# Two single PSUM banks in place of two halves of one tile, in a pool opened anew for each part

## The chip, the cores and the metric

One NeuronCore of a Trainium2 chip runs the whole program. The metric is the device time of one execution in microseconds, the median of three runs.

## What is computed

The reference chains three stages. An attention over 32 memory slots comes first (8 batches, 8 heads, 576 tokens, head width 64); its result is the input of two feed-forward layers in a row.

```python
a = exp(phi - max over tokens); a = a / (sum over tokens + 1e-9)
k_m = einsum('bhsm,bhsd->bhmd', a, k);  v_m = einsum('bhsm,bhsd->bhmd', a, v)
attn = softmax(q @ k_m.T / 8);          x = attn @ v_m          # 4608 tokens x 512
h = x @ moe_w_in;   x = (h * sigmoid(h)) @ moe_w_out            # 512 -> 2048 -> 512
h = x @ moe2_w_in;  x = elu(h) @ moe2_w_out                     # 512 -> 2048 -> 512
```

## The kernel before

All products are made on TensorE (PE); ACT and DVE empty PSUM, form the operands (most numbers are split into two float16 halves, so that one product is three matmuls, `mm3`, L1092) and do the pointwise work. The program has three parts.

- **The first steps**: a list of step names written out by hand (`FIRST`, run in the loop at L1850 to L1853) handles the first batch: its attention, the first weights, its first products.
- **Part 1** (`plan_first`, to about 675 us): the other batches' attention and the first feed-forward layer. A small planner (`Plan`) orders its steps by priorities, readiness and a table of costs, when the program is built; on the chip each engine then runs its own list in that order, and semaphores hold an instruction until what it needs is there.
- **Part 2** (a second `Plan`, from about 675 us to the end): the second feed-forward layer over nine blocks of 512 tokens, i = 0 to 8. For each block `plan_in2` runs eight steps, q = 0 to 7, each of seven products of six matmuls, and `plan_out2` runs the output products in two halves, e = 0 and 1. The planner mixes the in-products of one block with the out-products of the block before.

PSUM has eight banks. `ps_m` holds two double tiles, m0 and m1, in four of them; the pool `ps_a` holds the other four: a single tile with the tag a, one with the tag c, and one double tile with the tag u of shape [128, 2, 512], one bank for each half. `pair_tile` makes such a double tile. In part 1 the double tile serves as a third place for products (`ps_half` with 2, the name ph) and for the two halves of one product (`u_mm`, the name up).

In the first steps and in part 2 the same four banks are used singly, in turn. `a_tile` (L134) counts requests in `turn[0]`; requests 0 and 2 of every four get a new tile with the tag a or c, requests 1 and 3 get a view of the first or second half of a double tile named `both`, which is made once at the start (L153) and once more when part 2 begins (L1857):

```python
        k = turn[0] % 4
        turn[0] += turn[1]
        if turn[1]:
            if k % 2:
                v = both[0][:, k // 2, :n]
```

So in part 2 `both` is one tile all along, whose halves are written and read again and again, while a and c are new tiles on each request.

In part 2 a block's in-products use four banks, and the out-products the other four (`bank_tile`, L1488; a ring of four). Ring 1 is the pool `ps_o`, with four buffers of one tag; it is opened when `ps_m` has been closed (`open_ps_o`, L1484). Ring 0 is `a_tile`. Blocks with even i have their in-products in ring 0, those with odd i in ring 1.

One step q of `plan_in2` asks for two banks: A for four products, which ACT empties (`copy_c`, L1528), and D for three, which DVE empties with an addition (`add_c`, L1532). In an even block A is a tile a or c, called h2A in the trace, and D is a half of `both`: the first half for even q, the second for odd q. In an odd block A and D are tiles of `ps_o`, called h2A and h2D. The order of the products, copies and additions within a step is the same for both. The second product into D (index 6, `p7`) starts a new sum in the bank, and so waits for the addition that read the first (`c11`). Steps q and q+1 overlap in the plan, so that the two banks called D are in use at the same time.

Of the kernel before, what the change touches and what calls it, by code (L numbers as in the profile page):

```python
# [9 lines left out]
F32 = mybir.dt.float32  # L10
# [6 lines left out]
PSUM = bass.MemoryType.PSUM  # L17

P = 128
# [76 lines left out]
def attn_moe_moe(ctx: ExitStack, tc: tile.TileContext, qT, phiT, kvm, kvt, w1i, w1o, w2i, w2o, out):  # L96
# [9 lines left out]
    ps_a = ctx.enter_context(tc.tile_pool(name="ps_a", bufs=4, space=PSUM))  # L106
# [27 lines left out]
    def a_tile(shape, name, tag="a"):  # L134

        k = turn[0] % 4
        turn[0] += turn[1]
        if turn[1]:
            if k % 2:
                n = int(np.prod(shape[1:]))  # L140
                v = both[0][:, k // 2, :n]
                return v if len(shape) == 2 else v.rearrange(
                    "p (a b) -> p a b", a=shape[1]) if len(shape) == 3 else v.rearrange(
                    "p (a b c) -> p a b c", a=shape[1], b=shape[2])
            tag = "ac"[k // 2]
        return ps_a.tile(shape, F32, tag=tag, name=name, bufs=1)

    both = []

    def pair_tile(name):  # L150
        return ps_a.tile([P, 2, 512], F32, tag="u", name=name, bufs=1)

    both.append(pair_tile("both"))  # L153

    def col(name, n=1):
        return const.tile([P, n], F32, name=name)
# [546 lines left out]
    def mem_T(b, g):  # L703

        z = st[b]
        if g < NG:
            ps = z["eT", g] = a_tile([P, NC - 1, P], "eT", "c")
            for c in range(NC - 1):
                nc.tensor.transpose(ps[:, c], z["phi"][:, g, TAIL * g + c * P:TAIL * g + (c + 1) * P], ident)
        else:  # L710
            ps = z["eT", g] = a_tile([P, P], "etail", "c")
            nc.tensor.transpose(ps, z["phi"].rearrange("p g s -> p (g s)")[:, S - TAIL:S + TAIL], ident)
# [15 lines left out]
    def mem_kv(b, g, c):  # L728
        z = st[b]
        if (g, c) == (0, 0):  # L730
            z["kvp"] = a_tile([P, NG, P], "kvp", "c")
        t = z.pop(("kv", g, c))
        last = c == NC - 1
        for g in range(NG) if last else (g,):
            for h in range(4):
                m = slice(32 * h, 32 * h + 32)
                nc.tensor.matmul(  # L737
                    z["kvp"][m, g],
                    es_tail[:, g, m] if last else z["es"][:, (NC - 1) * g + c, m],
                    t[:, h * P:(h + 1) * P],  # L740
                    start=(g == 0 and c == 0 or g == 1 and last),
                    stop=(g == 0 and last or g == 1 and c == NC - 2),
                    tile_position=(0, 32 * h),
                )
# [646 lines left out]
    def plan_weights(pl, after, h_free):  # L1391

        for q in range(NRES + NRING):
            wi_load[q] = pl.load(896, 1, lambda q=q: load_wi(q, f"wi{q}" if q < NRES else "wi"), after)
            if q >= NRES:
                pl.ring("wi", NRING)
                wi_free[q] = pl.take("wi", wi_load[q])
        for n, j in enumerate(ORDER):
            deps = pl.ring("wr", 3) if n < 3 else h_free[(n - 3) // 2]
            wq_load[j] = [None, None]  # L1400
            for e in range(2):
                wq_load[j][e] = pl.load(512, 2, lambda n=n, e=e: load_wq(n, e), deps + wq_load[j][:e] + after)
            if n < 3:
                pl.take("wr", wq_load[j][0])
# [17 lines left out]
    def scale_tiles():  # L1422
        for name in ("mb", "mx", "am", "p_x", "pxw", "s_x", "s_g", "tmp"):
            sc[name] = ph2.tile([P, NB], F32, tag=name, name=name)
        for name in ("inv2", "io2"):
            sc[name] = ph2.tile([P, NB, 2], F32, tag=name, name=name)

    def x2_scales(a, e):


        n = e - a
        lo = [i * TB // S for i in range(a, e)]
        hi = [((i + 1) * TB - 1) // S for i in range(a, e)]
        mb, m, am, t = sc["mb"], sc["mx"], sc["am"], sc["tmp"]
        nb = hi[-1] + 1 - lo[0]
        nc.vector.tensor_reduce(out=mb[:, :nb], in_=mx_x2[:, lo[0]:lo[0] + nb], axis=AX.X, op=ALU.add)
        two_of = sum(u < v for u, v in zip(lo, hi))
        if two_of:
            tt(m[:, :two_of], mb[:, :two_of], mb[:, 1:two_of + 1], ALU.max)
        if two_of < n:  # L1440
            nc.vector.tensor_copy(m[:, two_of:n], mb[:, two_of:n])
        nc.gpsimd.partition_all_reduce(am[:, :n], m[:, :n], P, bass_isa.ReduceOp.max)
        r = slice(a, e)
        pow2sq(sc["p_x"][:, r], am[:, :n], t[:, :n])
        scaled_recip(sc["s_x"][:, r], sc["p_x"][:, r], 2.0 ** 12, t[:, :n])
        nc.vector.tensor_scalar(
            out=sc["pxw"][:, r], in0=sc["p_x"][:, r], scalar1=p_w2im, scalar2=None, op0=ALU.mult
        )
        scaled_recip(sc["s_g"][:, r], sc["pxw"][:, r], 2.0 ** 4, t[:, :n])
        for o, u, v, f in (("inv2", "p_x", p_w2i, 2.0 ** -24), ("io2", "pxw", p_w2o, 2.0 ** -16)):  # L1450
            for k in range(2):
                nc.vector.tensor_scalar(
                    out=sc[o][:, r, k], in0=sc[u][:, r], scalar1=v[:, k:k + 1], scalar2=f, op0=ALU.mult, op1=ALU.mult
                )

    def plan_x2(pl, i, rank):

        z = y[i]
        z["xh"] = [None] * (KD // 2)
        done = []  # L1460
        for k in range(KD // 2):
            load = pl.load(512, rank, lambda k=k: x2_tile(i, k), pl.ring("x", NX))
            free = pl.take("x", load)
            last = load
            for n in range(4):
                last = pl.add("DVE", COST["sum"], rank, lambda k=k, n=n: operands(z["x", k])[n](), [last])

            def hi(k=k):
                z["xh"][k] = ph2.tile([P, 2, 7, TQ], F16, tag=f"xh{k}", name=f"xh{i}_{k}")
                split_hi(z["xh"][k][:, 0], z["x", k][:, :B12], sc["s_x"][:, i:i + 1])  # L1470

            def lo(k=k):
                split_lo(z["xh"][k][:, 1], z["xh"][k][:, 0], z["x", k][:, :B12], sc["s_x"][:, i:i + 1])

            last = pl.add("ACT", COST["hi"], rank, hi, [last] + pl.ring(f"xh{k}", 1))
            z["xh_free", k] = pl.take(f"xh{k}", last)
            last = pl.add("DVE", COST["lo"], rank, lo, [last])
            free.append(last)
            done.append(last)
        z["xh_done"] = done  # L1480
# [367 lines left out]
    with tc.manual_schedule():  # L1848
        first = first_steps()
        turn[1] = 1  # L1850
        for name in FIRST.split():
            first.pop(name)()
        assert not first  # L1853
        turn[:] = 0, 0
        busy = plan_first()
        turn[1] = 1
        both[:] = [pair_tile("both")]  # L1857
        early.close()
        ph2 = ctx.enter_context(tc.tile_pool(name="ph2", bufs=1))
        scale_tiles()  # L1860
        nc.vector.tensor_reduce(out=p_w2im, in_=p_w2i, axis=AX.X, op=ALU.max)
        x2_scales(0, B - 1)
        pl = Plan(None, busy)
        last = st[B - 1]
        last["made"] = {}
        for n in range(NT):
            last["T_free", n] = pl.take("T", None)
        out1, squares, loads = plan_out1(
            pl, B - 1, 0, None, NT, {}, [], lambda: ph2.tile([P, 4, HS], F32, tag="y", name="y", bufs=2), ("y", 2), 1200)
        w1s_load = pl.gates["x"] = loads[4:5]  # L1870
        pl.gates[1] = [pl.add("PE", 0.0, 0, open_ps_o, out1)]
        for n in range(4, 7):
            pl.gates[f"t{5 + (tcount[0] + n) % NT}"] = last["T_free", n]
        made = last["made"]
        h_free = [made[T3, 0] + made[T3, 1] + made[T1, 0] + made[T1, 1], made[T4, 0] + made[T4, 1] + made[B22, 0] + made[B22, 1]]
        plan_x2(pl, 0, 0)
        plan_weights(pl, w1s_load, h_free)
        for i in range(NB):
            for q in range(KQ):
                plan_in2(pl, i, q)  # L1880
            plan_out2(pl, i, 0)
            if i == 2:
                pl.add("DVE", 2.5, 1000 * i + RANK["x2"], lambda: x2_scales(B - 1, NB), [y[i]["t_done", KQ - 1, 0]] + squares)
            if i + 1 < NB:
                plan_x2(pl, i + 1, 1000 * i + RANK["x2"])
            plan_out2(pl, i, 1)
        pl.run()
# [50 lines left out]
```

## Time and profile before

| | |
|---|---|
| median of three runs | 1367.56 us (1367.33 to 1369.19) |
| the profiled execution's own time | 1371.49 us |
| its span on the core | 1369.7 us |
| mean granted TensorE clock | 0.992 |
| PE busy | 97% of the span |
| DVE busy, ACT busy | 80%, 69% |
| part 2 | about 675 us to the end |

The span is the stretch from the first to the last instruction of one profiled execution; its own time is what a timer around that execution gives. A busy PE is one that has matmuls under way; the idle time in front of an instruction is put down to the semaphore event that came last. L1092 is the line of the helper `mm3`, which issues nearly all matmuls, so the rows are told apart by the tiles: out<-in, by the program's names without numbers, and `both` is the double tile whichever half is meant.

### The profile page before, as it was taken

Reading aid. Unit: us, or ns where it says so; the run is one execution under the profiler, and the core shown is the slowest. Engines: PE = TensorE matmul, PEld = TensorE weight load, DVE = VectorE, ACT = ScalarE, POOL = GpSimd, SP = SyncE. Lnnn points to the kernel's source line nnn. Section 1 sums busy time; section 2 is a strip of 40 time slices with the busy share of each in tenths; the row PEclk is TensorE's granted clock in tenths of the full one; section 3 lists DMA queues with packets and bytes.
Section 4 is the critical chain, followed back from the end, with each engine's and each line's share of the span. In section 5 each row is a group of like instructions: output and inputs, shape, how many; then the busy total and the mean of one; then the engine's idle time right before and its main releaser. Section 6 shows DMA issues by size and latency. Waiting matters only on the chain.

```text
span 1369.7 us, 28731 instructions
## 1 busy us (share of the span) xinstructions
PE 1335.2 (97%) x12089; PEld 1093.8 (80%) x12089; DVE 1102.5 (80%) x1731; ACT 951.1 (69%) x1374; POOL 85.3 (6%) x147
## 2 busy tenths in 40 slices
PE   8998999999999999999988999999999999999998
PEld 4676777777777776777877888888888888888887
DVE  7678887897979898898878696979787897869784
ACT  5767775868677796778486676858575867767672
POOL 0033100000001011011000000000000000000000
PEclk8999999999999999999999999999999999999999
DMA  9584777368657947635863151414232332414120
GB/s 390 192 265 137 268 277 271 120 234 276 209 198 236 335 145 256 241 135 200 346 215 112 53 172 44 152 50 147 74 124 85 113 112 77 148 43 166 58 97 32
DMA packets 65601, 233.07 MB, mean 170 GB/s; under 512 B 8896, under 2 KB 15040, under 8 KB 60864
## 3 DMA queue, kind: packets, MB, share of 16 engines
q1 hardware_dynamic: 52992, 187.19, 40.0%
q0 software_dynamic: 12480, 44.05, 8.5%
q8 instruction: 94, 1.54, 0.5%
q14 instruction: 35, 0.29, 0.1%
HBM read 186.12 MB, written 40.89 MB: 166 GB/s over the span
## 4 chain that ended last, share of the span: by engine, by line
PE 86%; DMA 5%; DVE 4%; ACT 3%; issue 1%; SPq 0%; POOL 0%; ACTq 0%; DVEq 0%; POOLq 0%
PE ph L1092 30%; PE o L1092 17%; PE h2A L1092 13%; PE both L1092 12%; PE h2D L1092 4%; PE up L930 2%; PE ph L1099 2%; PE ph L1138 2%; DMA w1i_hl<-w1i_hl 1%; PE sc L833 1%; DVE h L1532 1%; PE kvp L737 1%; DMA kv<-in_kvm 1%; DMA wi<-w2is 1%; DMA q<-in_qT 1%
## 5 line engine op out<-in xcount | busy, mean ns | idle before, releaser
L1092 PEld LDWEIGHTS <-wi 128*128 128x128 f16 x3024 | 296.2, 98 | 52.9 <-issue 13.2
L1092 PEld LDWEIGHTS <-wq 128*128 128x128 f16 x3024 | 295.7, 98 | 38.2 <-issue 3.7
L1092 PE MATMUL ph<-T,w1s 128*128 128x288 f16 x2352 | 302.0, 286 | 0.1
L1092 PEld LDWEIGHTS <-w1s 128*128 128x128 f16 x2352 | 227.5, 98 | 62.4 <-issue 6.5
L1092 PE MATMUL o<-t,wq 128*128 128x256 f16 x2160 | 273.2, 273 | 0.5 <-DVE t L206 0.4
L1092 PE MATMUL h2A<-xh,wi 128*128 128x256 f16 x1728 | 229.1, 274 | 5.3 <-DMA wi<-w2is 3.7
L1528 ACT ACTIVATE h<-h2A,inv 128x256 f32<-128x256 f32 x288 | 133.5, 469 | 141.3 <-PE h2A L1092 137.9
L206 DVE SCALAR_TENSOR_TENSOR t<-h,s_g,t 128x768 f16<-128x768 f32 (+1 forms) x144 | 163.7, 1146 | 10.1 <-ACT t L201 9.7
L1092 PE MATMUL ph<-aT,u 128*128 128x288 f16 x1344 | 167.3, 286 | 1.7 <-ACT h L1175 1.0
L201 ACT ACTIVATE t<-h,s_g 128x768 f16<-128x768 f32 (+1 forms) x144 | 146.4, 1034 | 24.8 <-DVE h L165 13.8
L1092 PEld LDWEIGHTS <-u 128*128 128x128 f16 x1344 | 130.9, 98 | 36.7 <-issue 3.9
L206 DVE SCALAR_TENSOR_TENSOR T<-h,c,T 128x1152 f16<-128x1152 f32 x98 | 137.5, 1413 | 22.9 <-ACT T L201 22.5
L165 DVE TENSOR_TENSOR h<-h 128x256 f32<-128x256 f32 (+1 forms) x302 | 129.4, 462 | 2.9
L201 ACT ACTIVATE T<-h,c 128x1152 f16<-128x1152 f32 x98 | 121.3, 1250 | 12.8 <-DVE h L165 7.0
L1092 PE MATMUL both<-t,wq 128*128 128x256 f16 x864 | 117.5, 272 | 1.5 <-DVE h L1532 1.2
L1532 DVE SCALAR_TENSOR_TENSOR h<-both,inv,h 128x256 f32<-128x256 f32 x120 | 56.8, 481 | 59.9 <-PE both L1092 52.0
L1092 PE MATMUL both<-xh,wi 128*128 128x256 f16 x720 | 96.2, 273 | 7.6 <-DVE h L1532 7.6
L1175 ACT ACTIVATE h<-ph,inv 128x576 f32<-128x576 f32 x112 | 81.9, 737 | 22.1 <-PE ph L1092 21.6
L1570 DVE SCALAR_TENSOR_TENSOR h<-e,h 128x1024 f32<-128x1024 f32 x72 | 87.7, 1218 | 7.1 <-ACT e L1566 7.1
L1563 ACT ACTIVATE e<-h 128x1024 f32<-128x1024 f32 x72 | 75.6, 1050 | 15.2 <-DVE h L1532 15.2
L1092 PE MATMUL h2D<-xh,wi 128*128 128x256 f16 x576 | 76.7, 273 | 0.0
L1566 ACT ACTIVATE e<-e 128x1024 f32<-128x1024 f32 x72 | 75.6, 1050 | 0.7
(214 smaller groups left out, 1437.9 us busy)
## 6 DMA issues: line engine op xcount, KB each, us to landing
w1s<-w1os SPq DMA_DIRECT2D x98, 512.0 KB, 4.5
wi<-w2is SPq DMA_DIRECT2D x56, 896.0 KB, 4.6
kv<-in_kvm SPq DMA_DIRECT2D x48, 256.0 KB, 5.4
q<-in_qT SPq DMA_DIRECT2D x32, 288.0 KB, 7.1
raw<-in_w1i SPq DMA_DIRECT2D x8, 1024.0 KB, 13.0
raw<-in_w1o SPq DMA_DIRECT2D x8, 1024.0 KB, 5.2
raw<-in_w2i SPq DMA_DIRECT2D x8, 1024.0 KB, 6.1
raw<-in_w2o SPq DMA_DIRECT2D x8, 1024.0 KB, 6.0
```

The source lines that it names most:

```text
L165: nc.vector.tensor_tensor(out=out, in0=a, in1=b, op=op)
L201: nc.scalar.activation(out=hi, in_=x, func=AF.Copy, scale=s)
L206: nc.vector.scalar_tensor_tensor(out=lo, in0=x, scalar=s, in1=hi, op0=ALU.mult, op1=ALU.subtract)
L930: nc.tensor.matmul(ps[c, :], z["vT"][:, i, g, c], wW[f][:, h % 2, 2 * g + h // 2], start=(i == 1), stop=(i == 0), tile_position=(0, 32 * h))
L1092: nc.tensor.matmul(o, w, x[:, c], start=first, stop=last, **how)
L1099: nc.tensor.matmul(o, w, x[:, c], start=(i == 0), stop=(i == n - 1))
L1175: nc.scalar.activation(out=h[m // KQ][:, :, m % KQ], in_=w.pop(m), func=AF.Silu, scale=z["inv1"][:, m // 4:m // 4 + 1])
L1528: nc.scalar.activation(out=w["x"][:, s], in_=w["A"], func=AF.Copy, scale=inv)
L1532: return pl.add("DVE", COST["add"], base, lambda: nc.vector.scalar_tensor_tensor(out=w["x"][:, s], in0=w["D"], scalar=inv, in1=w["x"][:, s ...
L1563: nc.scalar.activation(out=w["e"], in_=w["x"][:, B21:], func=AF.Relu, scale=-1.0)
L1566: nc.scalar.activation(out=w["e"], in_=w["e"], func=AF.Exp, scale=-1.0)
L1570: nc.vector.scalar_tensor_tensor(out=x, in0=w["e"], scalar=-1.0, in1=x, op0=ALU.add, op1=ALU.max)
```

## The change

The double tile leaves the pool `ps_a` for a pool of its own, `ps_u`, at the other end of PSUM. That pool is closed and opened anew for each part. In the first steps and in part 2 the requests 1 and 3 of `a_tile` now get new single tiles with the tags b and d from that pool, in place of a half of `both`; in part 1 the pool holds the double tile with the tag u as before. The order of the instructions, the planner's costs and the shapes stay as they are.

```diff
         k = turn[0] % 4
         turn[0] += turn[1]
+        pool = ps_a
         if turn[1]:
-            if k % 2:
-                n = int(np.prod(shape[1:]))
-                v = both[0][:, k // 2, :n]
-                return v if len(shape) == 2 else v.rearrange(
-                    "p (a b) -> p a b", a=shape[1]) if len(shape) == 3 else v.rearrange(
-                    "p (a b c) -> p a b c", a=shape[1], b=shape[2])
-            tag = "ac"[k // 2]
-        return ps_a.tile(shape, F32, tag=tag, name=name, bufs=1)
-
-    both = []
+            tag = "abcd"[k]
+            pool = ps_a if k % 2 == 0 else pair["pool"]
+        return pool.tile(shape, F32, tag=tag, name=name, bufs=1)
+
+    pair = {}
+
+    def open_pair():
+        if pair:
+            pair["open"].close()
+        pair["open"] = ctx.enter_context(ExitStack())
+        pair["pool"] = pair["open"].enter_context(tc.tile_pool(name="ps_u", bufs=1, space=PSUM, side="right"))
 
     def pair_tile(name):
-        return ps_a.tile([P, 2, 512], F32, tag="u", name=name, bufs=1)
-
-    both.append(pair_tile("both"))
+        return pair["pool"].tile([P, 2, 512], F32, tag="u", name=name, bufs=1)
+
+    open_pair()
...
         assert not first
         turn[:] = 0, 0
+        open_pair()
         busy = plan_first()
         turn[1] = 1
-        both[:] = [pair_tile("both")]
+        open_pair()
         early.close()
```

## Rows read from the trace of the kernel before

**Rows 1.** The page, busy time of the engines and their share of the span.

```profile
PE 1335.2 (97%) x12089; PEld 1093.8 (80%) x12089; DVE 1102.5 (80%) x1731; ACT 951.1 (69%) x1374; POOL 85.3 (6%) x147
```

**Rows 2.** The page, the chain that ended last, by engine.

```profile
PE 86%; DMA 5%; DVE 4%; ACT 3%; issue 1%; SPq 0%; POOL 0%; ACTq 0%; DVEq 0%; POOLq 0%
```

**Rows 3.** PE's waits by releaser in windows 675:755, 832:908, 984:1056: us, times, longest.

```profile
PE both L1092 <- DVE h L1532: 2.1, 4, 0.7
...
PE both L1092 <- DVE h L1532: 1.0, 2, 0.6
...
PE both L1092 <- DVE h L1532: 1.9, 3, 1.2
```

**Rows 4.** PE's waits in front of tile both, 670 us to the end: us, times.

```profile
  DVE h L1532: 8.7, 15
```

**Rows 5.** Windows 908:984 to 1132:1206: length, busy PE, PEld, DVE, ACT, POOL; PEclk.

```profile
908.00:984.00 76.00, 75.83 (x693) 67.56 (x692) 60.58 (x101) 53.46 (x77) 2.19 (x4) 1.00 0.31 102
984.00:1056.00 72.00, 70.12 (x637) 62.04 (x635) 59.06 (x99) 50.15 (x68) 2.18 (x4) 1.00 0.33 107
1056.00:1132.00 76.00, 76.00 (x697) 67.98 (x696) 61.73 (x102) 52.21 (x74) 2.17 (x4) 1.00 0.31 101
1132.00:1206.00 74.00, 72.11 (x655) 63.81 (x654) 59.63 (x99) 51.11 (x70) 2.18 (x4) 1.00 0.32 104
```

**Rows 6.** Groups of PE, 755 to 1282 us: count | busy us, mean ns | idle us, releaser.

```profile
L1092 PE MATMUL both<-t,wq 128*128 128x256 f16 x729 | 100.6, 272 | 0.9 <-DVE h L1532 0.6
L1092 PE MATMUL h2D<-xh,wi 128*128 128x256 f16 x576 | 76.7, 273 | 0.0
L1092 PE MATMUL both<-xh,wi 128*128 128x256 f16 x444 | 59.0, 272 | 4.2 <-DVE h L1532 4.2
```

**Rows 7.** Timeline around 1024 us: start, us, engine, line, tiles [idle before, releaser].

```profile
1022.46 0.82 PE L1092 MATMUL h2A<-xh,wi 128*128 128x256 f16 x6
...
1022.73 0.48 DVE L1532 SCALAR_TENSOR_TENSOR h<-both,inv,h 128x256 f32<-128x256 f32 x1 [0.81 <-PE both L1092]
...
1023.92 0.47 DVE L1532 SCALAR_TENSOR_TENSOR h<-both,inv,h 128x256 f32<-128x256 f32 x1
...
1024.45 0.82 PE L1092 MATMUL both<-xh,wi 128*128 128x256 f16 x6 [1.17 <-DVE h L1532]
```

**Rows 8.** The same timeline around 1031 us.

```profile
1030.54 0.48 DVE L1532 SCALAR_TENSOR_TENSOR h<-both,inv,h 128x256 f32<-128x256 f32 x1 [1.25 <-PE both L1092]
...
1031.61 0.48 DVE L1532 SCALAR_TENSOR_TENSOR h<-both,inv,h 128x256 f32<-128x256 f32 x1
...
1032.14 0.81 PE L1092 MATMUL both<-xh,wi 128*128 128x256 f16 x6 [0.33 <-DVE h L1532]
```

**Rows 9.** Timeline of the first steps, around 20 us and around 44 us.

```profile
18.25 0.69 DVE L165 TENSOR_TENSOR att<-both,smx 128x512 f32<-128x512 f32 x1
...
20.88 0.29 DVE L165 TENSOR_TENSOR att<-both,smx 128x128 f32<-128x128 f32 x1
...
21.23 1.08 PE L914 MATMUL both<-w1i,vT 64*32 64x256 f32 x8 [0.52 <-DVE att L165]
...
43.26 1.22 DVE L379 SCALAR_TENSOR_TENSOR w1i<-raw,w1i 128x1024 uint32<-128x1024 uint32 x1
...
44.91 0.15 PEld L914 LDWEIGHTS both<-w1i,vT 64*32 64x32 f32 x8 [0.39 <-DVE w1i L379]
```

**Rows 10.** The chain of block 0, in order of time: start, us, what.

```profile
718.77 0.67 PE both L1092 x6
719.46 6.66 DMA wi<-w2is
```

**Rows 11.** Timeline, PE's first product into a bank of `ps_o`.

```profile
698.60 0.82 PE L1092 MATMUL o<-t,wq 128*128 128x256 f16 x6
```

**Rows 12.** DMA issues, of the page and of 690:740: KB each, us to landing.

```profile
raw<-in_w1o SPq DMA_DIRECT2D x8, 1024.0 KB, 5.2
...
x2d<-y POOLq DMA_DIRECT2D x1, 576.0 KB, 11.2
```

## The prediction, made before the kernel was run

> **What bounds the kernel now.** I read the page's busy times first, then the chain, then PE's waits stretch by stretch. PE is busy for 97% of the span [rows 1] and makes up 86% of the chain that ended last [rows 2]. So a microsecond in which PE stands still is nearly a microsecond of the whole, and one saved on DVE or ACT is worth nothing unless PE waited for it. The change touches PSUM banks alone, so the question is which of PE's idle times hang on the double tile.
>
> In part 2 PE stood idle 15 times, 8.7 us in all, in front of a matmul into `both`, each time until a DVE addition of L1532 had ended [rows 4]. These waits fall into the even blocks, where D is a half of `both`: 2.1 us in block 0, 1.0 in block 2, 1.9 in block 4 [rows 3]; blocks 6 and 8 show the same 1.9 again, which adds up to 8.8 with the rounding, against the 8.7 of the one row. The odd blocks do the same products, copies and additions in the same order, with single tiles in their four banks, and 576 matmuls into h2D had 0.0 us of idle time in front of them; 444 matmuls of the same shape into `both` in the same stretch had 4.2 [rows 6]. The windows say it again: PE idles 1.9 us of 72 and 1.9 of 74 in the even blocks 4 and 6, and 0.2 and 0.0 of 76 in the odd blocks 3 and 5 [rows 5]. An odd block is thus a trial run of what the change makes of an even one.
>
> **Why the double tile waits.** Take the longest kind [rows 7]. PE ends its products into h2A at about 1023.28 (1022.46 + 0.82). Next in its list is step q = 6's second product into D, in the first half. The addition that empties that half runs from 1022.73 to 1023.21, so the bank is free before PE is. PE starts at 1024.45 all the same: it waits for the next addition, 1023.92 to 1024.39, which belongs to step 5 and reads the second half. Which half each side names is not in the rows; I read it from the kernel (even q, first half; odd q, second) and from the order of the instructions. I went through the 15 waits in this way: 12 wait for an addition that reads the other half, and for each of them the last reader of their own half was done by the time PE was free. So the wait hangs on the tile as a whole, not on the bank.
>
> The other three are the 0.33 us waits of blocks 4, 6 and 8 [rows 8]. There PE does wait for its own half (the addition at 1031.61), but that addition is late because the one before it, at 1030.54, had waited 1.25 us for a product into the other half. They go with the same cause.
>
> **The change, part by part.**
>
> - *Single tiles b and d in part 2.* Removes the 15 waits: 8.7 us [rows 4]. What is late next? In the odd blocks nothing is [rows 5, 6]; there DVE and ACT are busy for 61 and 52 to 53 us of 76 [rows 5], so they can follow a PE that comes a little sooner. In block 0 PE also waits for transfers of weights; the one on the chain is issued at 719.46, right after the products into `both` that end at 719.44 and free its buffer [rows 10], so it moves with PE and takes nothing back. I take all 8.7; the lower bound is the first rival's 8.7 - 3.5 - 2.1 = 3.1.
> - *Out-products in `both`.* Beside 0.6 us that is in the 8.7 already, 0.3 us of idle time stood before them between 755 and 1282 us [rows 6]. With single tiles I take the 0.3 as gone; bounds 0 and 0.3.
> - *Single tiles in the first steps.* One wait of the same kind, 0.52 us at 21.23: the matmul writes the half that the subtraction at 18.25 had read by 18.94, and waits for the one at 20.88, which reads the other half [rows 9]. What follows on PE moves along at most until 44.91, where a weight load waits for a conversion that ends at 44.48 [rows 9]; so about 0.4 us can be kept there, and later stretches of the chain are DMA [rows 2], which may not move. I take 0.2; bounds 0 and 0.4.
> - *Part 1.* The pool holds the double tile as before, and its waits stay. Nothing is gained or lost.
> - *Opening the pool twice.* The trace has one such event: `ps_m` is closed and `ps_o` opened in its banks, and PE's first product there has no idle time in front of it [rows 11]. The new tiles' banks were last read long before they are next written. I take 0. The upper bound is what still travels when a pool is opened: one load of first-layer weights, 5.2 us, at the first opening and one store of 11.2 us at the second [rows 12], 16.4 us together, if all engines had to wait for it. Nothing below 0 is possible, since no instruction goes away.
> - *Other banks.* Tiles move to other bank numbers. Matmuls of one shape last 272 or 273 ns in `both` and in h2D, which lie in different banks [rows 6]: 0. The granted clock is 1.00 in even and odd blocks alike [rows 5], the level of 2.4 GHz, so there is no term for it.
> - *Queues.* No instruction is moved past another, no DMA is added, no queue is reordered.
>
> Sum: 8.7 + 0.3 + 0.2 = 9.2 us off. The profiled execution took 1371.5 us, so it would take 1362.3; the median of the runs lies 3.9 us below it (its span is 1369.7), so the same 9.2 off the median of 1367.6 gives **1358.4 us**.
>
> **The rivals.**
>
> 1. *Part of the gain comes back as other waits.* At the three waits of 1.17 us in blocks 4, 6 and 8 DVE runs without a break from 1023.92 to past 1024.45 [rows 7]; if PE comes 1.2 us sooner and the next product then needs an addition that DVE has not reached, 3 x 1.2 = 3.5 us return. Block 0, which has few out-products to fill in with, may give back its 2.1 [rows 3], and the first steps their 0.2. What is left is 8.7 + 0.3 - 3.5 - 2.1 = 3.4, so 1364.2 us. The 0.0 in the odd blocks [rows 6] speaks against it; that block 0 has no odd counterpart speaks for it.
> 2. *Nothing changes, because the waits are a matter of too few banks.* The bubbles repeat, three to a block. Then four banks hold the next product up whichever tile they are cut from, and the change, which adds no bank, leaves 1367.6 us. The odd blocks speak against it: four banks, and 0.0 us of idle time [rows 6]. The Trainium skill's page "Perfetto Trace Analysis", section "Optimization Strategy", reads a gap that repeats on the engine that should be saturated as a possible lack of SBUF or PSUM for the next tile. By that rule the change is worth nothing; the trace does not agree with it for this gap.
> 3. *Slower: opening a pool holds the program up.* If each opening makes every engine wait until all that is under way has landed, it costs up to 5.2 + 11.2 = 16.4 us [rows 12], against 9.2 gained: 1374.8 us. The place is the end of the first steps and the start of part 2; it decides once the two openings cost more than 9.2 us together. [Rows 11] speak against it.
>
> **How the numbers follow.** The forecast gets 0.70, the first rival 0.16, the second 0.09, the third 0.05. The predicted time is the forecast's, 1358.4. The range begins at 1357.0, which is the forecast with all bounds at their best (8.7 + 0.3 + 0.4 = 9.4, so 1358.2) and 1.2 us for the scatter of the median (the three runs lie 1.9 us apart); it ends at 1364.5, just past the first rival. About 0.8 lies in it. A measurement of this kernel can tell some 0.2%, 2.7 us, from no change: faster means below 1364.8. The forecast and nearly all of the first rival lie there, 0.84; the second rival and the rest of the first make 0.11 for no change; the third makes 0.05 for slower.
>
> **What the profile of the changed kernel would show.** If right: no PE wait of more than 0.2 us in front of D's products in the even blocks (their tile is then called h2D there too, 1296 matmuls in all with about 0.0 idle), PE busy for all but some 0.2 us of each block from 2 on, the wait at 21 us gone, and part 2 starting at nearly the same time as before. The forecast is wrong if the same waits stand in front of the single tiles (second rival), if waits of PE for ACT, DVE or weights grow in the even blocks (first rival), or if PE or the DMA queues stand still around 60 us or 675 us (third rival).

## The result, and the profile after

The changed kernel takes 1353.80 us (median; four runs, 1351.77 to 1354.85) where the kernel before took 1367.45 us beside it: a ratio of 0.9896, with an interval from 0.9881 to 0.9912. That is 13.7 us less, where 9.2 had been forecast; the time lies below the range (1357.0 to 1364.5). The direction, the place and the cause were right, the size was not.

The profiled execution took 1354.85 us, with a span of 1353.1 and a mean granted clock of 0.995. The page's busy times and the chain by engine, which answer to [rows 1] and [rows 2]:

```profile
PE 1327.9 (98%) x12089; PEld 1092.9 (81%) x12089; DVE 1101.8 (81%) x1731; ACT 950.2 (70%) x1374; POOL 85.2 (6%) x147
```

```profile
PE 88%; DMA 4%; DVE 3%; ACT 3%; issue 1%; POOL 0%; SPq 0%; ACTq 0%; DVEq 0%; POOLq 0%
```

DVE and ACT do the same work as before to within 1 us. The 16.6 us by which this span is shorter than the one before are PE's: its waits, and 7 us of "busy" time, of which more below.

PE's matmuls into D, the group on the page (count | busy, mean ns | idle us in front), and all that PE waits for from 670 us on (us, times, longest), which answers to [rows 3, 4, 6]:

```profile
L1094 PE MATMUL h2D<-xh,wi 128*128 128x256 f16 x1296 | 174.1, 274 | 0.0
```

```profile
PE h2A L1094 <- DMA wi<-w2is: 4.1, 3, 2.1
PE h2A L1094 <- ACT h L1530: 1.0, 2, 0.6
```

All 1296 matmuls into D now go by the name h2D, and none shows idle time in front of it. The list of PE's waits has lost its longest entry, and no other has come in its place.

The windows of the even blocks 4 and 6, to be read beside [rows 5] (length, busy PE, PEld, DVE, ACT, POOL; PEclk):

```profile
970.00:1042.00 72.00, 72.00 (x661) 64.40 (x659) 59.26 (x99) 51.56 (x72) 2.18 (x4) 1.00 0.32 107
...
1116.00:1189.00 73.00, 73.00 (x672) 65.41 (x670) 59.85 (x101) 51.61 (x72) 2.18 (x4) 1.00 0.32 105
```

PE is busy in all of 72 and of 73 us, where 1.9 us were missing in each.

And the place of [rows 7], now at 1013 us (timeline: start, us, engine, line, tiles):

```profile
1012.50 0.48 DVE L1534 SCALAR_TENSOR_TENSOR h<-h2D,inv,h 128x256 f32<-128x256 f32 x1
...
1013.21 0.82 PE L1094 MATMUL h2A<-xh,wi 128*128 128x256 f16 x6
...
1013.69 0.48 DVE L1534 SCALAR_TENSOR_TENSOR h<-h2D,inv,h 128x256 f32<-128x256 f32 x1
1013.87 0.82 PE L1094 MATMUL h2D<-xh,wi 128*128 128x256 f16 x6
```

PE starts its six matmuls into h2D 0.66 us after the six into h2A, at 1013.87, while the addition that held it up before (1013.69 to 1014.17) is still under way: it reads another tile now.

### The profile page after: what moved, and what is told of

Same layout as the page of the kernel before. It is cut to its first block, busy times and chain, and to the rows that moved or that the text cites. A ratio compares the mean times of both kernels' runs of the same rounds, so it can differ in the third digit from the quotient of the medians.

```text
span 1353.1 us, 28725 instructions
## 1 busy us (share of the span) xinstructions
PE 1327.9 (98%) x12089; PEld 1092.9 (81%) x12089; DVE 1101.8 (81%) x1731; ACT 950.2 (70%) x1374; POOL 85.2 (6%) x147
## 4 chain that ended last, share of the span: by engine, by line
PE 88%; DMA 4%; DVE 3%; ACT 3%; issue 1%; POOL 0%; SPq 0%; ACTq 0%; DVEq 0%; POOLq 0%
PE ph L1094 31%; PE o L1094 24%; PE h2A L1094 14%; PE h2D L1094 10%; PE up L932 2%; PE ph L1101 2%; PE ph L1140 1%; PE sc L835 1%; DMA w1i_hl<-w1i_hl 1%; PE kvp L739 1%; DMA kv<-in_kvm 1%; DMA wi<-w2is 1%; DMA q<-in_qT 1%; PE up L916 0%; PE aTp L887 0%
## 5 line engine op out<-in xcount | busy, mean ns | idle before, releaser
L1094 PE MATMUL o<-t,wq 128*128 128x256 f16 x3024 | 358.4, 273 | 0.1
L208 DVE SCALAR_TENSOR_TENSOR t<-h,s_g,t 128x768 f16<-128x768 f32 (+1 forms) x144 | 163.9, 1146 | 13.8 <-ACT t L203 13.5
L1094 PE MATMUL h2D<-xh,wi 128*128 128x256 f16 x1296 | 174.1, 274 | 0.0
L1534 DVE SCALAR_TENSOR_TENSOR h<-h2D,inv,h 128x256 f32<-128x256 f32 x216 | 103.6, 481 | 79.0 <-PE h2D L1094 56.1
L208 DVE SCALAR_TENSOR_TENSOR T<-h,c,T 128x1152 f16<-128x1152 f32 x98 | 137.5, 1412 | 22.7 <-ACT T L203 22.2
L1177 ACT ACTIVATE h<-ph,inv 128x576 f32<-128x576 f32 x112 | 82.0, 737 | 22.2 <-PE ph L1094 22.0
L167 DVE TENSOR_TENSOR h<-h,h 128x1152 f32<-128x1152 f32 x42 | 56.7, 1353 | 11.7 <-ACT h L1177 11.5
L1140 PE MATMUL ph<-h,w1o 128*128 128x288 f32 x256 | 65.2, 411 | 0.5 <-DVE w1o L381 0.5
```

The source lines that it names most:

```text
L167: nc.vector.tensor_tensor(out=out, in0=a, in1=b, op=op)
L208: nc.vector.scalar_tensor_tensor(out=lo, in0=x, scalar=s, in1=hi, op0=ALU.mult, op1=ALU.subtract)
L1094: nc.tensor.matmul(o, w, x[:, c], start=first, stop=last, **how)
L1140: nc.tensor.matmul(z[d][1][t], wB[d][:, k], h[k // KQ][:, t, k % KQ], start=(k == 0), stop=(k == KF - 1))
L1177: nc.scalar.activation(out=h[m // KQ][:, :, m % KQ], in_=w.pop(m), func=AF.Silu, scale=z["inv1"][:, m // 4:m // 4 + 1])
L1534: return pl.add("DVE", COST["add"], base, lambda: nc.vector.scalar_tensor_tensor(out=w["x"][:, s], in0=w["D"], scalar=inv, in1=w["x"][:, s ...
```

## Where the other 4.5 us were: what a wait costs

In block 5 PE was busy all the time and issued 697 matmuls in 76.00 us [rows 5]: they start 0.109 us apart, and six of them take 0.66 us from start to start. But a row shows each of them for 0.273 us and six of them for 0.82: by the rows a matmul is still running when the next one starts. (The profile models the ends of matmuls; nothing below rests on them but the idle time that it shows.) The idle time in front of an instruction is counted from the end of the row before it. A matmul that could have started 0.109 us after the one before, and starts 0.273 us after it, has lost 0.164 us and shows no idle time at all; a longer wait loses 0.164 us more than it shows. In [rows 7] PE's products start at 1022.46 and 1024.45, 1.99 us apart in place of 0.66: 1.33 us are lost, where 1.17 are shown.

The short kind can be seen in the timeline of the kernel before:

```profile
1007.57 0.82 PE L1092 MATMUL h2A<-xh,wi 128*128 128x256 f16 x6
1008.38 0.82 PE L1092 MATMUL both<-xh,wi 128*128 128x256 f16 x6
1009.03 0.82 PE L1092 MATMUL h2A<-xh,wi 128*128 128x256 f16 x6
```

and the same three products in the changed kernel:

```profile
998.48 0.82 PE L1094 MATMUL h2A<-xh,wi 128*128 128x256 f16 x6
999.13 0.82 PE L1094 MATMUL h2D<-xh,wi 128*128 128x256 f16 x6
999.79 0.82 PE L1094 MATMUL h2A<-xh,wi 128*128 128x256 f16 x6
```

The product into `both` starts 0.81 us after the one before it and has no bracket of idle time; the one into h2D starts after 0.65. 0.15 us were lost with nothing shown.

The Trainium skill's page "Trainium Kernel Development and Optimization", section "Performance Expectations", calls the busy time of matmuls a bad metric for how close a kernel is to roofline, because matmuls are pipelined. The trace agrees that busy time hides losses: of the 13.9 us lost in e3, below, 4.8 were counted as busy.

So I counted the loss from the starts: for each matmul of 256 columns in part 2 the time since the start of the one before it, less 0.109 us, where that is more than 0.025. The table has, for most of the kernels, the matmuls into D and the out-products that lie in the double tile (or in its successor):

| kernel | idle shown, us | lost by starts, us | times (with no idle shown) |
|---|---|---|---|
| before | 9.0 | 14.2 | 37 (19) |
| changed, into h2D | 0.0 | 1.5 | 14 (14) |
| e1, into h2D | 0.0 | 0.2 | 2 (2) |
| e2 | 9.0 | 13.9 | 34 (16) |
| e3 | 9.0 | 13.9 | 33 (15) |
| e4, the double tile under A and D | 18.3 | 26.0 | 54 (14) |
| e5, the double tile of the odd blocks | 6.8 | 11.0 | 29 (13) |

For e3 the sum is 9.0 shown, 18 times 0.1637 = 2.9 that these 18 waits don't show, and 1.9 in 15 waits that don't show at all. In the profiles of before and changed some matmuls lost 0.10 us each for another reason, a low clock in block 0 (last section).

A second count does without the 0.109 us. PE's 12089 matmuls come in the same order in before, changed, e0, e3 and e5, so each can be compared with its counterpart: by how much does it start earlier? From the second block on, this lead grows by 10.6 us from before to changed: by 11.0 at the matmuls whose tile had been the double one, and by -0.3 at all others together. From e3 to e0 it grows by 11.9 us, 11.0 of them at those matmuls. From the second block on, before shows 6.9 us of idle time at them and loses 11.0 by the starts.

## The experiments

Two theories stood against each other. A: the waits of part 2 cost what the starts say, 13.9 us, and that is the whole gain. B: part 2 gives its 9 us of visible idle time, the other 4.5 come from the first steps and part 1 (in the profiles, the changed kernel was 2.5 us ahead at 128 us). C, a third, was that the tiles' move to other banks did it.

**e1, single tiles in part 2 alone.** `open_pair` got a flag, with which the pool gives one double tile for the requests 1 and 3, as before.

```diff
+            if k % 2 and "both" in pair:
+                v = pair["both"][:, k // 2, :n]
...
-    open_pair()
+    open_pair(True)
...
-        open_pair()
+        open_pair(False)
```

> The first steps keep one double tile (from the new pool), part 2 gets the single tiles. Theory A (the waits of part 2 cost more than the idle time shown in front of them, because a stall also lays bare the last matmul before it: 0.27 us in its row, while the next may start 0.11 us after it): all but 0.3 to 0.7 us of the gain stays, 1353 to 1355 us, and part 2 is 13.5 to 14 us shorter than before. Theory B (part 2 gives only the 9 us of its visible idle time, the other 4.5 come from the first steps and part 1): 1358 us. Theory C (the gain beyond 9 us comes with the move to other banks): as A, it does not tell these apart.

Measured: 1355.22 us, ratio 0.9918 (0.9893 to 0.9943); nine of the ten runs lie between 1351.30 and 1358.58, one at 1367.35. The wait of the first steps is there as before:

```profile
PE both L925 <- DVE att L176: 0.5, 1, 0.5
```

From the second block's first product to PE's last matmul it took 597.7 us, the kernel before 609.4 (1364.9 - 755.5). With block 0, which scatters (below), part 2 was 17.6 us shorter in this profile, more than the 13.5 to 14 expected. The gain is part 2's, as A had it; the median is 0.2 us above A's span, and its interval leaves B's 1358 (0.994) just inside. What decides against B is e2.

**e2, single tiles in the first steps alone** (the same kernel with the two flags exchanged).

> The single tiles in the first steps alone, part 2 keeps the double tile. Theory A: 0.3 to 0.7 us faster than before at most, 1366.7 to 1367.5, with the wait of 0.5 us at 21 us gone and the 15 waits of part 2 as before. Theory B: 4 to 5 us faster, 1363.

Measured: 1367.02 us, ratio 1.0004 (0.9991 to 1.0017). No gain that can be measured, and B's 4 to 5 us are excluded. In part 2 the waits are those of [rows 4]:

```profile
  DVE h L1543: 8.7, 15
```

**e3, the pool alone** (both flags on: banks and openings of the changed kernel, tiles of the one before).

> The pool of its own, opened three times, at the other end of PSUM, but with the double tile wherever it was: banks and openings change, tiles don't. Theories A and B: the time of before, 1367.5 within 0.5 us, 15 waits and 8.7 us of idle time in front of the double tile. Theory C (banks): 4 to 5 us faster than before. If the openings cost anything: slower than before.

Measured: 1368.17 us, ratio 1.0001 (0.9985 to 1.0017), and the same row of 8.7 us, 15 times. Three openings and the move to other banks cost nothing and give nothing that can be measured (the interval leaves some 2 us either way); C, which wanted 4 to 5 us, falls, and so does the third rival of the prediction.

**e4, another pair under the double tile.** The double tile lies under A and D of the even steps, the banks of the odd steps are single.

```diff
-            if k % 2 and "both" in pair:
-                v = pair["both"][:, k // 2, :n]
+            if k < 2 and "both" in pair:
+                v = pair["both"][:, k, :n]
```

> In part 2 the double tile lies under the two banks of one step (A and D of the even steps); the banks of the odd steps are single tiles. Theory A (it is the tile that PE waits for, whichever engine reads it): D's products now wait for ACT's copies out of A and A's for DVE's additions, within a step, so waits of PE in front of the double tile on both ACT and DVE, and slower than the changed kernel by 5 to 25 us, 1359 to 1379. If it were a matter of D and DVE alone, or of two steps that overlap: no waits, 1354.

Measured: 1380.62 us, ratio 1.0102 (1.0077 to 1.0127), 27 us above the changed kernel's 1353.80 and 25 above e1 beside it, somewhat past the span that I gave. PE's idle time in front of the double tile from 670 us on (us, times):

```profile
  ACT h L1539: 9.9, 18
  DVE h L1543: 7.1, 12
  ACT u L1664: 0.5, 1
```

Now it waits for ACT's copies out of A as well, which it never did in front of D. The engine that reads does not matter, the tile does: two banks cut from one tile hold each other up. That they do so more here than before fits their being used closer together in time, which no run varied by itself. The size fits theory A again: this double tile lost 26.0 us by the starts, where 18.3 are shown.

**e5, the fault put where it never was.** The changed kernel, with a double tile under every second bank of `ps_o`, the odd blocks' ring.

```diff
+        ps["two"] = ps["o"].tile([P, 2, 512], F32, tag="two", name="two", bufs=1)
...
-            return ps["o"].tile([P, 2, TQ], F32, tag="o", name=name, bufs=4)
+            k = ps["n"] % 4
+            ps["n"] += 1
+            if k % 2:
+                return ps["two"][:, k // 2].rearrange("p (a b) -> p a b", a=2)
+            return ps["o"].tile([P, 2, TQ], F32, tag="o", name=name, bufs=2)
```

> The changed kernel, but with a double tile for every second bank of the odd blocks' ring: the fault of before put where it never was. From 755 us on, the even blocks of before lost 6.9 us by the idle time shown in front of the double tile and 11.0 us by the intervals between the starts of the matmuls. Theory A (the intervals count): 11 us (8 to 13) slower than the changed kernel, about 1365; the profile shows about 6 to 8 us of idle time in front of the double tile, and intervals that add up to 0.16 us more for each wait. Theory B (the idle time counts): 7 us slower, 1361. If odd blocks are safe for another reason: 1354.

Measured: 1364.32 us, against 1352.55 for the changed kernel on the same chip (e0): 11.8 us slower. The groups of PE from 749 to 1280 us (count | busy, mean ns | idle us, releasers):

```profile
L1094 PE MATMUL two<-t,wq 128*128 128x256 f16 x622 | 85.2, 272 | 2.0 <-DVE h L1540 1.2 <-DVE v L167 0.6
L1094 PE MATMUL two<-xh,wi 128*128 128x256 f16 x576 | 76.7, 272 | 4.5 <-DVE h L1540 3.9 <-DVE u L167 0.6
L1094 PE MATMUL h2D<-xh,wi 128*128 128x256 f16 x444 | 59.1, 273 | 0.0
```

The odd blocks now have the waits and the even ones none, [rows 6] the other way round. 6.5 us are shown here, 6.8 in all of part 2; 11.0 are lost by the starts, and the median rose by 11.8. The times alone don't exclude 7 us, since e0's four runs lie between 1351.70 and 1358.08; the profiles do. From the second block's first product to the last matmul e5 takes 608.9 us, and changed, e0 and e7 take 597.7 to 598.8, which is 10 to 11 us less. Matmul by matmul, the lead from e5 to e0 grows by 11.1 us there, 11.0 of them at the matmuls into `two`. This settles the size: 7 us (1361) had been the mark of a theory that counts idle time.

**e0 and e7, the changed kernel again.**

> The changed kernel once more, for its scatter (four runs lay between 1351.8 and 1354.9). Theory A: 1351.5 to 1355; runs with a higher mean granted clock are the shorter ones, and part 2 takes the same time in each profile within 1 us.

> The changed kernel beside the next one on the same chip. Its earlier ratios to the kernel before were 0.990 and 0.991: the same here, 1351 to 1355 us.

Measured: 1352.55 us, ratio 0.9913 (0.9886 to 0.9940), and 1355.51 us, ratio 0.9913 (0.9893 to 0.9933). The gain over the kernel before is thus between 11.4 and 13.7 us in three comparisons. From the second block to the last matmul the profiles of changed, e0 and e7 take 598.8, 597.7 and 597.8 us; those of before, e2 and e3 609.4, 608.5 and 609.7. There the gain is 10 to 12 us, 11 in the mean. Block 0 is what scatters: 71.7 to 75.3 us with single tiles in part 2 (changed, e0, e1, e7), 74.2 to 77.7 without (before, e2, e3). So the expectation that part 2 takes the same time within 1 us failed: it took 673.3, 669.4 and 673.0 us in changed, e0 and e7. The median of e7 lies 0.5 us past the span expected. The expectation that shorter runs have the higher clock held for e0 (0.997, span 1349.9) but says little for e7 (0.996, span 1355.3).

**e6 and e8, a version that beats both.** What PE still waits for in part 2 is mostly the weights wi. One resident and three rotating buffers in place of two and two:

```diff
-    NX, NRES, NRING = 3, 2, 2
+    NX, NRES, NRING = 3, 1, 3
```

> The changed kernel with one resident and three rotating weight buffers (wi) in part 2 in place of two and two, since what PE still waits for in its part 2 is mostly these loads (3 to 5 us in block 0 and one of 0.9 at block 7). Not about the tiles: it asks what bounds part 2 now. If the loads' late start is the cause, 1 to 4 us less than the changed kernel (1349 to 1352); if the transfers themselves are slow there, or the new order of loads delays others, no change or a few us more.

> Three rotating weight buffers once more, beside the changed kernel. If the loads of block 0 and of block 7 start sooner, 1 to 3 us less than the run beside it, the waits of PE for wi below 1.5 us in all; if the 0.988 of before was scatter, within 0.5 us of the run beside it.

Measured: 1351.42 us, ratio 0.9882 (0.9853 to 0.9910), as expected but not clear of the changed kernel's 0.9896; then, beside e7, 1348.99 us, ratio 0.9863 (0.9837 to 0.9889), four runs from 1347.86 to 1350.44 where e7's six lay between 1353.38 and 1357.50. PE's waits in part 2 of e7 and of e8 (us, times, longest):

```profile
PE h2A L1094 <- DMA wi<-w2is: 4.3, 2, 3.2
PE h2A L1094 <- ACT h L1530: 1.0, 2, 0.6
```

```profile
PE h2A L1094 <- ACT h L1530: 1.5, 3, 0.6
PE h2A L1094 <- DMA wi<-w2is: 0.4, 1, 0.4
```

The wait of 3.2 us is gone, and 6.5 us with it, more than twice what I had thought likely. Part 2 is 5.3 us shorter in these two profiles (673.0 and 667.7 us from its first to its last matmul), 3.9 of them the wait; behind the long wait the clock is low, as the last section shows, and in e8 it is not. How much the third buffer is worth depends on how block 0 went in the kernel beside it: against e0's 669.4 us part 2 is 1.7 us shorter.

## Why the prediction was wrong in size and right in cause

- *"Removes the 15 waits: 8.7 us."* This step failed. The waits went, all of them, and none came back (first fence of PE's waits above); but 8.7 us is the idle time that the view shows, and the time that PE lost was 13.9 by the starts. The sum should have had 9.0 shown, 2.9 hidden in the waits that show and 1.9 in the waits that don't. *"PE ends its products into h2A at about 1023.28"* took the end of a row for the time from which PE could go on; from start to start six matmuls take 0.66 us, so that was 1023.12. The signs were in the rows quoted: 697 matmuls in 76.00 us [rows 5], 0.109 us each, where one lasts 272 or 273 ns [rows 6], and 1.99 us between two starts in [rows 7].
- *"What is late next? In the odd blocks nothing is"*. Right, and the odd blocks were the trial run that they were taken for: the even blocks 4 and 6 now keep PE busy without a gap.
- *The transfer in block 0 "moves with PE and takes nothing back".* Not shown either way: the wait for wi is 3.7, 0.8 and 2.8 us in the profiles with the double tile (before, e2, e3) and 4.1, 4.3, 1.8 and 1.4 in those with single tiles (changed, e7, e0, e1), so it scatters by more than block 0 had to give. The starts gave 2.8 to 2.9 us for block 0 (e3, e2; 3.2 in before, with the low clock); what of it reaches the end differs from run to run.
- *The out-products' 0.3 us* are in the 9.0 and were gone.
- *The first steps, 0.2 us.* Not to be told from nothing (e2). PE did come sooner there, and gave most of it back: in the changed kernel

```profile
21.55 2.12 PE L1686 MATMUL idle<-h 128*128 128x512 f16 x8
...
25.04 0.63 PE L887 MATMUL aTp<-ident,att 128*128 128x128 f32 x4 [0.94 <-DVE att L167]
...
29.01 1.07 PE L916 MATMUL up<-w1i,vT 64*32 64x256 f32 x16 [0.45 <-DVE w1i L381]
```

  the wait at 21 us became a wait of 0.94 us for the attention weights and one of 0.45 for a conversion of weights, both made by DVE. At 31 us PE was 0.7 us ahead of the kernel before in this profile and 0.8 and 1.0 in e2 and e0, but 0.4 and 1.1 behind in e5 and e7, where the granted clock was 0.50 once more from 26 and 27 us on.
- *Part 1, the openings, the other banks: 0.* Right, within the 2 us that e3 can tell.
- *The rivals.* Returned waits, too few banks and costly openings: none came true. The rule on repeating gaps in the Trainium skill's page "Perfetto Trace Analysis", section "Optimization Strategy", which stood beside the second rival, names a possible cause that was not the cause of this gap: the number of banks is the same and the gap is gone.
- *The range* was drawn around the wrong sum; its lower end left 1.2 us for scatter, and no bound for the size of a wait itself.
- *Luck.* That the first comparison gave 13.7 us, so near to the 13.9 of the starts, is in part luck: the other two gave 13.4 and 11.4. What the profiles agree on is the 11 us from the second block on.

Left open: whether PE's own wait for the other half or DVE's (which also waited for products into the other half, [rows 8]) counts for more. No run took one of them away alone. In [rows 7] both are there: PE could have gone on at 1023.12 (1022.46 + 0.66), and its own half was being read until 1023.21, by an addition that had itself stood 0.81 us for a product into the tile. The three waits of the second kind lost 0.49 us each by the starts, 1.5 of the 13.9.

## What to carry to other kernels

In a program like this one, banks that are used singly should be single tiles: a tile is what the waits are written for, and two banks cut from one tile wait for each other's readers, whichever engine reads (e4) and wherever they lie (e5). And a wait of PE is to be sized from the starts of its matmuls, not from the idle time in front of them: in a stream of matmuls of 256 columns each wait costs 0.16 us more than it shows, and those under 0.16 us show nothing.

## What the runs showed of the hardware that I had not expected

A short wait is dearer than its length if the clock falls behind it. In the kernel before PE stood still for 2.98 us in front of 726 us. Two windows of it, from there on (length, busy PE, PEld, DVE, ACT, POOL; PEclk):

```profile
726.00:729.00 3.00, 2.84 (x14) 2.03 (x15) 0.37 (x1) 0.06 (x1) 0.00 (x0) 0.50 0.00 0
729.00:735.00 6.00, 6.00 (x56) 5.34 (x55) 4.57 (x9) 4.81 (x8) 0.00 (x0) 0.99 0.47 153
```

and of the changed kernel, after a wait of 2.13 us that ended at 720.65:

```profile
721.00:725.00 4.00, 4.00 (x25) 2.92 (x23) 2.02 (x3) 1.57 (x3) 0.00 (x0) 0.59 0.14 20
725.00:730.00 5.00, 5.00 (x47) 4.44 (x46) 4.34 (x9) 3.82 (x6) 0.00 (x0) 0.98 0.44 168
```

The granted clock is 0.50 and 0.59 there, the level of 1.2 GHz for all or most of the stretch, and matmuls start 0.21 us apart in place of 0.11: some 15 starts in either kernel lost 0.10 us each, 1.5 us on top of the wait. PE counts as busy all the while. In e7, 3.22 us that ended at 724.16 were followed by a clock of 0.62 from 724 to 728 us. In e0, e1 and e5, whose block 0 took 71.6 to 71.8 us, the wait at this place was 0.9 to 1.1 us, in e2 and e3 0.8 and 1.9, in e8 there was none, and in all six no such stretch follows. Whether the length of the wait decides it, no run here tested.

The first steps show what the lower level costs, too: the same eight matmuls into `idle` took 2.12 us in the changed kernel (granted 0.88 from 21.5 to 23.6 us) and 3.60 in the one before (0.50 from 22.2 to 25.7). And around 120 us the stretch of nine microseconds behind PE's longest wait (3.9 and 3.7 us) was granted 0.62 in the profile of before and 0.83 in that of the changed kernel:

```profile
118.00:127.00 9.00, 7.63 (x35) 5.70 (x37) 8.86 (x15) 7.20 (x12) 1.59 (x3) 0.62 0.30 119
```

```profile
118.00:127.00 9.00, 8.73 (x74) 6.55 (x75) 8.97 (x13) 6.87 (x13) 2.42 (x4) 0.83 0.30 119
```

Sixteen matmuls there took 6.36 us before and 4.97 after. That is 1.4 of the 2.5 us of lead at 128 us on which theory B was built; 1.1 were there when the long wait ended. And e3, with the double tile wherever it had been, was 1.3 us ahead of before at the same place, so this lead says little of the tiles. It is one more reason why two spans (16.6 us apart) differ by more than two medians (13.7).
